# Top-k attention and SwiGLU block on one Trainium2 core: a parametric ReLU on ScalarE as the mask, normalization on GpSimd

## The chip, the cores and the metric

The kernel runs on one core of a Trainium2 chip. The metric is the device time of one execution in microseconds (us); lower is better. The engines are called by their short names: PE (TensorE, matrix products), ACT (ScalarE), DVE (VectorE), POOL (GpSimd) and SP (which issues most transfers).

## What is computed

Attention over 8 batches and 8 heads, 576 queries and keys of 64 numbers, in which each query keeps only its 32 highest scores, and then a SwiGLU feed-forward block (FFN) over the 4608 tokens. All in float32.

```python
# attention, q, k, v: (8, 8, 576, 64)
scores = scale * np.matmul(q, k.transpose(0, 1, 3, 2))      # scale = 1/8
kth = np.partition(scores, -32, axis=-1)[..., -32:-31]
scores = np.where(scores >= kth, scores, -1e9)
attn = np.exp(scores - scores.max(-1, keepdims=True))
attn = attn / (attn.sum(-1, keepdims=True) + 1e-9)
x = np.matmul(attn, v)                                      # to (4608, 512)
# FFN, w_gate and w_val (512, 1536), w_out (1536, 512)
g = x @ w_gate
out = (g * (1 / (1 + np.exp(-g))) * (x @ w_val)) @ w_out
```

## The kernel before

The attention is cut into 160 units: one unit is a batch, a tile of 128 queries and a pair of heads. 128 units have two heads of 128 queries each; in the last query tile of a batch (64 queries) both heads share the 128 partitions, so those 32 units count as one head. The order is by batch, then query tile, then pair of heads.

Each unit passes through these steps, all of them functions of the kernel:

- `scores` (L278): PE multiplies queries and keys into four PSUM banks (tile `s`, L308; L294 for the short units); ACT copies them to SBUF (tile `sc`, L313, L299).
- `select` (L316): for each head DVE takes the eight highest values four times (MAX8, L328) and between these rounds overwrites the ones found (MATCH_REPLACE8, L332). The 32 values stand in tile `m`, the 32nd in its last column. Then one instruction for each head compares the scores with that 32nd value and writes a penalty of -3e38 or 0 into tile `e` (L338).
- `penalize` (L342): POOL makes the bias of exp from the highest score (L348) and adds scores and penalty (L350).
- `weigh` (L353): ACT takes exp with the sum as a second output (L359) and adds a small constant to the sum, tile `tot` (L364).
- `normalize` (L367): DVE takes the reciprocal of the sum (L371), and ACT multiplies by it (L374).
- `turn` (L376): PE transposes the weights (tile `etps`, L386) and ACT copies them to `et` (L387).
- `values` (L397): PE multiplies with `v` for two units at once (tile `av`, L420); ACT copies the result into the FFN's input `xT` (L436).

The FFN is `feed` (L462), a generator that yields after each small piece of PE's work. It goes through 18 blocks of 256 tokens. Gate and value products (tile `f`, L476) go to PSUM; ACT evaluates them (L501 to L503, L508); POOL multiplies (L504, L509). The output product has two forms: a plain one for the first block (L522) and one of seven quarter products for the others (L562), with sums and differences on POOL (L548, L569, L577, L582, L610). A block can begin only when the attention of all its 256 tokens is done. The FFN's weights come in 36 pieces that are rounded on the way: a transfer that SP issues (L106), ACT (L114 to L117), DVE (L121), POOL (L122, L123).

The order on every engine is fixed by hand: at its end the kernel ties each instruction to the one before it on the same engine, so an engine never overtakes. That order is written by the main loop (L747), whose step n belongs to unit n. On DVE it runs `select(n)`. Around it stand `penalize(n - 1)` and `weigh(n - 1)`, `turn(n - 2)`, and in even steps the scores of units n + 1 and n + 2 and the values of units n - 4 and n - 3. The reciprocal of unit n - 1 comes at the end of step n, and the multiplication by it at the front of step n + 1, ahead of the copies of scores. Between these, `pieces` takes pieces of the FFN against a credit that `share` gives each step, and `dve` runs selection instructions and, with them, steps of the weights' rounding. All PSUM tiles of the attention (`s`, `av`, `etps`, `kqps`) share five banks in rotation; the FFN has three. `sc` and `e` have three buffers each, `m` two.

Of the kernel before, what the change touches and what calls it, by code (L numbers as in the profile page):

```python
# [8 lines left out]
AF = mybir.ActivationFunctionType  # L9
ALU = mybir.AluOpType  # L10
FP32 = mybir.dt.float32
# [4 lines left out]
P = 128  # L16
TOP_K = 32
LOWEST = -3.4028234663852886e38
FAR = -3.0e38
EPS = 1.0e-9  # L20
BLK = 256
WP = 256
# [3 lines left out]
def kernel(  # L26
# [66 lines left out]
    for i in range(NV):  # L93
        vt = consts.tile([P, P], FP32, name=f"vlast{i}")
        nc.vector.memset(vt[:], 0.0)
        vlast.append(vt)
    eps = consts.tile([P, 1], FP32, name="eps")
    nc.vector.memset(eps[:], EPS)
    wg = consts.tile([P, KC, DFF], FP32, name="wg")
    wv = consts.tile([P, KC, DFF], FP32, name="wv")  # L100
    wo = consts.tile([P, MC, DM], FP32, name="wo")
# [176 lines left out]
    def scores(n):  # L278
        b, qt, hp = units[n]
        slab = preps[b * NHP + hp]  # L280
        sc = work.tile([P, 2 * S], FP32, tag="sc", name="sc", bufs=3)
        halves = [slice(0, D), slice(D, P)]
        half = S // 2

        def bank():
            return ps_t.tile([P, 512], FP32, tag="t", name="s")


        if qt == J:
            banks = [bank() for _ in range(2)]  # L290
            for i, ps in enumerate(banks):
                for d in halves:
                    k0 = R + i * half
                    nc.tensor.matmul(  # L294
                        ps[d, 0:half], slab[d, S + R : S + 2 * R], slab[d, k0 : k0 + half]
                    )
            yield
            for i, ps in enumerate(banks):
                nc.scalar.copy(sc[:, i * half : (i + 1) * half], ps[:, 0:half])  # L299
        else:  # L300
            q0 = S + 2 * R + qt * P
            banks = []
            for i in range(2):
                for hh, d in enumerate(halves):
                    ps = bank()
                    banks.append((i + 2 * hh, ps))
                    k0 = (1 - hh) * R + i * half
                    nc.tensor.matmul(  # L308
                        ps[:, 0:half], slab[d, q0 : q0 + P], slab[d, k0 : k0 + half]
                    )  # L310
            yield
            for i, ps in banks:
                nc.scalar.copy(sc[:, i * half : (i + 1) * half], ps[:, 0:half])  # L313
        state[n] = dict(sc=sc)

    def select(n):  # L316

        nh = n_heads(units[n][1])
        sc = state[n]["sc"]
        m = small.tile([P, 2, TOP_K], FP32, tag="m", name="m", bufs=2)  # L320
        heads = [slice(t * S, (t + 1) * S) for t in range(nh)]
        e = work.tile([P, 2 * S], FP32, tag="e", name="e", bufs=3)
        state[n] |= dict(m=m, e=e, heads=heads)
# [2 lines left out]
        for r in range(rounds):  # L326
# [3 lines left out]
            if r < rounds - 1:  # L330
# [3 lines left out]
                    )  # L334
                    yield
                cur = e
        for t, hs in enumerate(heads):
            nc.vector.tensor_scalar(  # L338
                e[:, hs], sc[:, hs], m[:, t, TOP_K - 1 : TOP_K], FAR, ALU.is_lt, ALU.mult
            )  # L340

    def penalize(n):  # L342

        st = state[n]
        sc, m, e, heads = st.pop("sc"), st.pop("m"), st["e"], st["heads"]
        nh = len(heads)
        bias = small.tile([P, 2], FP32, tag="bias", name="bias")
        nc.gpsimd.tensor_scalar_mul(bias[:, 0:nh], m[:, 0:nh, 0], -scale)  # L348
        for hs in heads:
            nc.gpsimd.tensor_tensor(e[:, hs], e[:, hs], sc[:, hs], ALU.add)  # L350
        st["bias"] = bias

    def weigh(n):  # L353

        st = state[n]
        e, heads, bias = st["e"], st["heads"], st.pop("bias")
        tot = small.tile([P, 2], FP32, tag="tot", name="tot")
        for t, hs in enumerate(heads):
            nc.scalar.activation(  # L359
                e[:, hs], e[:, hs], AF.Exp, bias=bias[:, t : t + 1], scale=scale,  # L360
                accum_out=tot[:, t : t + 1],
            )
        nh = len(heads)
        nc.scalar.activation(tot[:, 0:nh], tot[:, 0:nh], AF.Identity, bias=eps[:])  # L364
        st["tot"] = tot

    def normalize(n):  # L367
        st = state[n]
        tot, e, heads = st.pop("tot"), st["e"], st.pop("heads")
        nh = len(heads)  # L370
        nc.vector.reciprocal(tot[:, 0:nh], tot[:, 0:nh])  # L371
        yield
        for t, hs in enumerate(heads):
            nc.scalar.mul(e[:, hs], e[:, hs], tot[:, t : t + 1])  # L374

    def turn(n):  # L376

# [340 lines left out]
    def pieces(n):  # L718
        for _ in range(n):
            if credit[0] >= 1:  # L720
                credit[0] -= piece()

    def run(steps):
        for _ in steps:
            pass
# [15 lines left out]
    load(2)  # L741
    credit = [0.0]
    no = iter(())
    scaled = no
    TURN = 2
    due = [2.0]
    for n in range(NU + 3):  # L747
# [6 lines left out]
        def dve(k, beside=True):  # L754

            for _ in range(k * nh):
                next(topk, None)
                due[0] += 5 / 6 if beside else 0
                if due[0] >= 1:
                    due[0] -= 1  # L760
                    rounding(1)
# [4 lines left out]
            credit[0] = min(credit[0] + share(n), share(n) + 1)  # L766
        flush(on_act)
        if 0 <= n - 1 < NU:
            penalize(n - 1)
        flush(on_pool)  # L770
        run(scaled)
        if nxt:
            run(nxt.pop(0))
        if valued(n):
# [27 lines left out]
        next(ahead, None)  # L802
        dve(1)
        pieces(1)
        dve(2, beside=False)
        run(topk)
        next(norm, None)
        scaled = norm
        pieces(6)
    while piece():  # L810
        pass
# [48 lines left out]
```

## Time and profile before

| | us |
|---|---|
| median of three runs (1789.26 to 1791.48) | 1791.11 |
| the profiled execution | 1790.76 |
| its span, first to last instruction | 1788.7 |
| PE busy | 1686.3 (94%) |
| DVE busy | 1619.7 (91%) |
| ACT busy | 1209.5 (68%) |
| POOL busy | 1068.0 (60%) |
| mean granted PE clock | 0.966 |

Busy time is the time in which an engine has an instruction in work, over the whole span. PE's granted clock is between 0.64 and 0.74 in the first 150 us, 0.93 from 300 to 400 us, and 0.98 or more in nearly all the rest. In the chain of work that ended last, 81% of the span are PE's, 9% DVE's and 4% POOL's. The transfers take little: 59.67 MB in all, 33 GB/s in the mean.

A row of the profile names the line of the kernel, the engine, the operation, and its tiles as output<-input, with shapes in partitions x elements. In a table of groups there follow busy time, mean ns of one instruction, and how long the engine was idle just before these, with what ended most of that idle time. In a timeline a row begins with its start and its length in us, and the number in brackets is the idle time before it.

### The profile page before, as it was taken

Reading aid. Unit: us, or ns where it says so; the run is one execution under the profiler, and the core shown is the slowest. Engines: PE = TensorE matmul, PEld = TensorE weight load, DVE = VectorE, ACT = ScalarE, POOL = GpSimd, SP = SyncE. Lnnn points to the kernel's source line nnn. Section 1 sums busy time; section 2 is a strip of 40 time slices with the busy share of each in tenths; the row PEclk is TensorE's granted clock in tenths of the full one; section 3 lists DMA queues with packets and bytes.
Section 4 is the critical chain, followed back from the end, with each engine's and each line's share of the span. In section 5 each row is a group of like instructions: output and inputs, shape, how many; then the busy total and the mean of one; then the engine's idle time right before and its main releaser. Section 6 shows DMA issues by size and latency. Waiting matters only on the chain.

```text
span 1788.7 us, 30860 instructions
## 1 busy us (share of the span) xinstructions
PE 1686.3 (94%) x11012; PEld 1396.2 (78%) x11012; DVE 1619.7 (91%) x3372; ACT 1209.5 (68%) x2881; POOL 1068.0 (60%) x1058
## 2 busy tenths in 40 slices
PE   4458999799999999999999999999999999999999
PEld 3337678588888888888888878888888878888877
DVE  7999999999999999999999989999999999999400
ACT  6788776667667677667666776767676776676431
POOL 4878856455565646564656646566556555756434
PEclk7669999899999999999999999999999999999989
DMA  7433030001200030001200030000300020000000
GB/s 193 126 96 95 32 75 14 13 1 36 60 1 13 3 80 15 12 1 35 62 13 1 13 71 26 1 13 6 90 1 13 1 55 15 13 1 13 1 12 12
DMA packets 109306, 59.67 MB, mean 33 GB/s; under 512 B 88544, under 2 KB 96992, under 8 KB 109152
## 3 DMA queue, kind: packets, MB, share of 16 engines
q1 hardware_dynamic: 108016, 57.37, 12.3%
q8 instruction: 87, 1.43, 0.3%
q14 instruction: 67, 0.55, 0.1%
q10 hardware_dynamic: 1136, 0.33, 0.1%
HBM read 48.23 MB, written 9.44 MB: 32 GB/s over the span
## 4 chain that ended last, share of the span: by engine, by line
PE 81%; DVE 9%; POOL 4%; ACT 3%; issue 2%; DMA 0%; SPq 0%; POOLq 0%; ACTq 0%; DVEq 0%
PE f L476 39%; PE x_ps L562 9%; PE av L420 8%; PE s L308 7%; PE etps L386 6%; PE y_ps L562 6%; DVE m L328 4%; DVE e L332 4%; PE s L294 2%; POOL e L350 1%; PE kqps L263 1%; PE o_ps L522 1%; DVE e L338 1%; DVE size L121 1%; ACT e L359 1%
## 5 line engine op out<-in xcount | busy, mean ns | idle before, releaser
L328 DVE MAX8 m<-e 128x8 f32<-128x576 f32 x864 | 614.5, 746 | 3.3
L350 POOL TENSOR_TENSOR e<-e,sc 128x576 f32<-128x576 f32 x288 | 408.7, 1437 | 111.8 <-DVE e L338 53.8
L332 DVE MATCH_REPLACE8 e<-m,e 128x576 f32<-128x576 f32 x576 | 423.3, 741 | 0.0
L476 PE MATMUL f<-xT,wg 128*128 128x256 f32 x1728 | 405.6, 384 | 0.0
L476 PE MATMUL f<-xT,wv 128*128 128x256 f32 x1728 | 399.6, 380 | 0.0
L476 PEld LDWEIGHTS f<-xT,wg 128*128 128x128 f32 x1728 | 326.4, 192 | 52.2 <-issue 8.9
L476 PEld LDWEIGHTS f<-xT,wv 128*128 128x128 f32 x1728 | 323.0, 190 | 49.1 <-issue 7.9
L504 POOL TENSOR_TENSOR h<-h,half_g 128x512 f32<-128x512 f32 x108 | 139.0, 1287 | 284.1 <-ACT h L503 274.5
L359 ACT ACTIVATE e<-e,bias 128x576 f32<-128x576 f32 x288 | 222.8, 778 | 79.0 <-POOL e L350 79.0
L509 POOL TENSOR_TENSOR h<-h,val 128x512 f32<-128x512 f32 x108 | 139.4, 1291 | 148.7 <-ACT val L508 147.9
L386 PE MATMUL etps<-ident,e 128*128 128x128 f32 (+1 forms) x1312 | 184.0, 284 | 45.7 <-ACT e L374 37.5
L374 ACT ACTIVATE e<-e,tot 128x576 f32<-128x576 f32 x288 | 210.9, 781 | 20.9 <-DVE tot L371 20.8
L308 PE MATMUL s<-kqT 64*128 64x288 f32 x1024 | 181.4, 461 | 41.9 <-ACT sc L313 27.6
L386 PEld LDWEIGHTS etps<-ident,e 128*128 128x128 f32 (+1 forms) x1312 | 157.5, 145 | 76.6 <-ACT e L374 41.4
L387 ACT COPY et<-etps 128x512 f32<-128x512 f32 (+1 forms) x448 | 182.5, 483 | 44.1 <-PE etps L386 44.0
L332 DVE MATCH_REPLACE8 e<-m,sc 128x576 f32<-128x576 f32 x288 | 211.5, 740 | 0.0
L328 DVE MAX8 m<-sc 128x8 f32<-128x576 f32 x288 | 202.5, 739 | 9.1 <-ACT sc L313 9.1
L338 DVE TENSOR_SCALAR e<-sc,m 128x576 f32<-128x576 f32 x288 | 185.4, 680 | 1.1
L313 ACT COPY sc<-s 128x288 f32<-128x288 f32 x512 | 164.9, 407 | 17.0 <-PE s L308 16.8
L308 PEld LDWEIGHTS s<-kqT 64*128 64x128 f32 x1024 | 102.6, 198 | 89.6 <-ACT sc L313 33.0
L420 PE MATMUL av<-et,v 128*64 128x128 f32 (+1 forms) x2560 | 158.6, 267 | 0.0
L501 ACT ACTIVATE h<-f 128x512 f32<-128x512 f32 x108 | 64.3, 595 | 116.8 <-PE f L476 116.6
(73 smaller groups left out, 2045.9 us busy)
## 6 DMA issues: line engine op xcount, KB each, us to landing
v<-in_v_dram SPq DMA_DIRECT2D x32, 256.0 KB, 3.2
kq_in<-in_k_dram SPq DMA_DIRECT2D x63, 128.0 KB, 2.9
kq_in<-in_q_dram SPq DMA_DIRECT2D x63, 128.0 KB, 3.1
w<-in_moe_w_gate_dram SPq DMA_DIRECT2D x12, 512.0 KB, 3.9
w<-in_moe_w_val_dram SPq DMA_DIRECT2D x12, 512.0 KB, 3.7
w<-in_moe_w_out_dram SPq DMA_DIRECT2D x12, 512.0 KB, 3.6
out_dram<-o SPq DMA_DIRECT2D x38, 128.0 KB, 2.4
out_dram<-o SPq DMA_DIRECT2D x16, 256.0 KB, 2.4
```

The source lines that it names most:

```text
L308: nc.tensor.matmul(ps[:, 0:half], slab[d, q0 : q0 + P], slab[d, k0 : k0 + half])
L328: nc.vector.max(m[:, t, 8 * r : 8 * r + 8], cur[:, hs])
L332: nc.vector.match_replace(e[:, hs], m[:, t, 8 * r : 8 * r + 8], cur[:, hs], LOWEST)
L338: nc.vector.tensor_scalar(e[:, hs], sc[:, hs], m[:, t, TOP_K - 1 : TOP_K], FAR, ALU.is_lt, ALU.mult)
L350: nc.gpsimd.tensor_tensor(e[:, hs], e[:, hs], sc[:, hs], ALU.add)
L359: nc.scalar.activation(e[:, hs], e[:, hs], AF.Exp, bias=bias[:, t : t + 1], scale=scale, accum_out=tot[:, t : t + 1],)
L374: nc.scalar.mul(e[:, hs], e[:, hs], tot[:, t : t + 1])
L386: nc.tensor.transpose(ps[0:kl, c * P : (c + 1) * P], e[:, k0 : k0 + kl], ident[:])
L387: nc.scalar.copy(et[0:kl, c0 : c0 + cn, :], ps[0:kl, 0 : cn * P].rearrange("p (c j) -> p c j", c=cn),)
L420: nc.tensor.matmul(av[d, i, 0:ql], weights_, moving, start=c == (0 if last else J), stop=c == (J if last else J - 1),)
L476: nc.tensor.matmul(ps[:, i, :], w[:, kc, m * P : (m + 1) * P], x[:, kc, :], start=(kc == 0), stop=(kc == KC - 1),)
L562: nc.tensor.matmul(ps, lhsT, T[i][m], start=m == 0, stop=m == MQ - 1)
```

## The change

A score x with the 32nd highest score t of its row is turned into t - x by ACT's input scaling, which is zero or negative where x is kept and positive where it is not. The parametric ReLU leaves positive values as they are and multiplies negative ones by 2^-90. exp then takes -2^90 times the result with a bias of t minus the highest score: kept scores come out as x minus the highest, and the others so far down that exp gives zero. The scale of 1/8 moves into the copies of scores.

With that, the comparison on DVE (L338), the addition on POOL (L350) and the constant's addition on ACT (L364) go. Two Prelu per unit come in on ACT ahead of exp; an addition of the constant for each head comes in on DVE ahead of the reciprocal; the multiplication by the reciprocal moves from ACT to POOL, with the reciprocal as a broadcast operand. In the main loop, the whole of `normalize(n - 1)` now runs within step n, ahead of the last two replacements and maxima of `select(n)`; before, its DVE part came at the end of step n and its multiplication at the front of step n + 1. POOL's bias instruction subtracts instead of multiplying. `m` gets three buffers. PE's instructions and their order stay as they are.

```diff
-FAR = -3.0e38
+SMALL = 2.0**-90
...
-    eps = consts.tile([P, 1], FP32, name="eps")
-    nc.vector.memset(eps[:], EPS)
...
# scores(n), in both branches
-                nc.scalar.copy(sc[:, i * half : (i + 1) * half], ps[:, 0:half])
+                nc.scalar.mul(sc[:, i * half : (i + 1) * half], ps[:, 0:half], scale)
...
# select(n)
-        m = small.tile([P, 2, TOP_K], FP32, tag="m", name="m", bufs=2)
+        m = small.tile([P, 2, TOP_K], FP32, tag="m", name="m")
...
-        for t, hs in enumerate(heads):
-            nc.vector.tensor_scalar(
-                e[:, hs], sc[:, hs], m[:, t, TOP_K - 1 : TOP_K], FAR, ALU.is_lt, ALU.mult
-            )
...
-    def penalize(n):
+    def shift(n):
...
-        nc.gpsimd.tensor_scalar_mul(bias[:, 0:nh], m[:, 0:nh, 0], -scale)
-        for hs in heads:
-            nc.gpsimd.tensor_tensor(e[:, hs], e[:, hs], sc[:, hs], ALU.add)
+        nc.gpsimd.tensor_tensor(
+            bias[:, 0:nh], m[:, 0:nh, TOP_K - 1], m[:, 0:nh, 0], ALU.subtract
+        )
...
# weigh(n)
         for t, hs in enumerate(heads):
             nc.scalar.activation(
-                e[:, hs], e[:, hs], AF.Exp, bias=bias[:, t : t + 1], scale=scale,
+                e[:, hs], sc[:, hs], AF.Prelu, bias=m[:, t, TOP_K - 1 : TOP_K], scale=-1.0,
+                alpha=SMALL,
+            )
+        for t, hs in enumerate(heads):
+            nc.scalar.activation(
+                e[:, hs], e[:, hs], AF.Exp, bias=bias[:, t : t + 1], scale=-1.0 / SMALL,
                 accum_out=tot[:, t : t + 1],
             )
-        nh = len(heads)
-        nc.scalar.activation(tot[:, 0:nh], tot[:, 0:nh], AF.Identity, bias=eps[:])
...
# normalize(n)
+        for t in range(nh):
+            nc.vector.tensor_scalar_add(tot[:, t : t + 1], tot[:, t : t + 1], EPS)
         nc.vector.reciprocal(tot[:, 0:nh], tot[:, 0:nh])
         yield
         for t, hs in enumerate(heads):
-            nc.scalar.mul(e[:, hs], e[:, hs], tot[:, t : t + 1])
+            nc.gpsimd.tensor_tensor(
+                e[:, hs], e[:, hs], tot[:, t : t + 1].to_broadcast([P, S]), ALU.mult
+            )
...
# the main loop
         if 0 <= n - 1 < NU:
-            penalize(n - 1)
+            shift(n - 1)
         flush(on_pool)
-        run(scaled)
         if nxt:
             run(nxt.pop(0))
...
         next(ahead, None)
         dve(1)
         pieces(1)
+        run(norm)
         dve(2, beside=False)
         run(topk)
-        next(norm, None)
-        scaled = norm
         pieces(6)
```

## The prediction

> **What bounds the kernel now.** I read the page's busy table first, then the table by stretches of time, then the timeline where that table shows TensorE idle. The busy table leaves two candidates:
>
> ```profile
> PE 1686.3 (94%) x11012; PEld 1396.2 (78%) x11012; DVE 1619.7 (91%) x3372; ACT 1209.5 (68%) x2881; POOL 1068.0 (60%) x1058
> ```
>
> The stretches separate them (columns: stretch, its length, busy us of PE, PEld, DVE, ACT, POOL, clock, DMA share, GB/s). I chose the cuts where PE fills up (137), runs dry (328) and fills up again (356).
>
> ```profile
> 0.00:137.00 137.00, 67.46 (x364) 46.90 (x364) 125.06 (x260) 102.23 (x227) 96.40 (x85) 0.68 0.51 139
> 137.00:328.00 191.00, 185.21 (x1158) 145.93 (x1158) 186.18 (x376) 141.60 (x331) 138.14 (x125) 0.98 0.17 48
> 328.00:356.00 28.00, 16.44 (x129) 11.95 (x128) 28.00 (x62) 17.42 (x48) 10.52 (x11) 0.81 0.05 20
> 356.00:1650.00 1294.00, 1285.96 (x8632) 1078.84 (x8633) 1257.08 (x2634) 901.88 (x2181) 760.48 (x773) 1.00 0.09 23
> ```
>
> Read it so: until 137 us, PE is half idle and DVE is never idle once it has data. There is no finished attention block, so PE has no FFN product to run, and DVE's selection sets the pace. From 356 to 1650 us, PE idles 8.0 of 1294 us while DVE idles 37. After DVE has ended, PE works alone for some 90 us. So PE sets the end, and time is to be won only where PE starves: 69.5 us idle in the first stretch, 5.8 in the second, 11.6 in the third.
>
> Next, what ends the starving in the first and the third stretch (the number in brackets is the engine's idle time before the row):
>
> ```profile
> 135.20 1.80 DVE L338 TENSOR_SCALAR e<-sc,m 128x576 f32<-128x576 f32 x2
> 136.92 0.15 DVE L371 RECIPROCAL tot<-tot 128x2 f32<-128x2 f32 x1
> 137.11 1.44 ACT L374 ACTIVATE e<-e,tot 128x576 f32<-128x576 f32 x2 [0.63 <-DVE tot L371]
> 138.46 1.28 ACT L313 COPY sc<-s 128x288 f32<-128x288 f32 x4
> 138.89 2.59 PE L308 MATMUL s<-kqT 64*128 64x288 f32 x8 [4.46 <-ACT sc L313]
> 141.40 4.94 PE L476 MATMUL f<-xT,wg 128*128 128x256 f32 x16
> ...
> 352.30 1.44 ACT L374 ACTIVATE e<-e,tot 128x576 f32<-128x576 f32 x2 [5.67 <-DVE tot L371]
> 354.07 1.71 PE L308 MATMUL s<-kqT 64*128 64x288 f32 x8 [3.63 <-ACT sc L313]
> ```
>
> One chain, twice: mask (L338), reciprocal at the loop's end (L371), ACT's multiplication (L374), the copies of scores behind it in ACT's queue (L313) that free PSUM banks, PE's next scores, and only then the first FFN product. The change removes the first link and moves the second and third.
>
> **What the Trainium skill says.** "ScalarE: Activation LUTs", What ACT_TABLE_LOAD costs: an ACTIVATE with a pointer bias takes about 280 + 0.833 N ns whatever the function, 760 ns at N = 576. The trace agrees: L359 (exp) 778 ns, L374 781 ns. "SBUF — State Buffer", Who interferes with whom: tensor_scalar can take the port pair that DVE shares with GpSimd, and the second comer blocks. The trace agrees: L338 takes 490 to 1611 ns, median 512, mean 680. "GPSIMD Engine Reference", 3.1: two-input elementwise work costs about 2.6 cycles per element, by my estimate 576 x 2.6 / 1.2 GHz = 1250 ns and a dispatch; L350 shows 1437 ns. "Perfetto Trace Analysis", Identifying the Most-Contended Engine, warns that matmul busy time is a poor measure of headroom. So I checked starts: the 16 products from 923.65 us give way to the next group at 927.21, 0.22 us each, and long runs of L476 elsewhere keep 0.216. PE really is full there.
>
> **The change, part by part.** The rows used:
>
> ```profile
> L350 POOL TENSOR_TENSOR e<-e,sc 128x576 f32<-128x576 f32 x288 | 408.7, 1437 | 111.8 <-DVE e L338 53.8
> L359 ACT ACTIVATE e<-e,bias 128x576 f32<-128x576 f32 x288 | 222.8, 778 | 79.0 <-POOL e L350 79.0
> L374 ACT ACTIVATE e<-e,tot 128x576 f32<-128x576 f32 x288 | 210.9, 781 | 20.9 <-DVE tot L371 20.8
> L338 DVE TENSOR_SCALAR e<-sc,m 128x576 f32<-128x576 f32 x288 | 185.4, 680 | 1.1
> ```
>
> *DVE.* Gone are 288 masks, 185.4 us. Added are 288 additions on 128x1. No such row exists; the nearest is the reciprocal on 128x1, 156 ns, behind which the next instruction starts after 0.08 us (136.92 to 137.00). A loop of two heads then pays 0.08 + 0.16 + 0.08 = 0.3 us for two additions and a reciprocal that waits for them; bounds 0.2 and 0.6. Before, mask to next loop took 1.80 us in even and about 1.15 in odd loops (135.20 to 137.00; 122.38 to 123.54), mean 1.47. Net: 1.17 us per loop, and ten loops (units 0 to 9) lie before the first FFN product. **Gain in stretch one: 11.7 us.** DVE's total should fall to about 1460 us; from 356 us on that buys nothing, since PE is the cover that hides it.
>
> *ACT.* Gone: 288 multiplications (210.9) and 160 Identity additions of eps (47.3). Added: 288 Prelu, taken as 778 ns (bounds 700 and 900), 224 us. Copies that become multiplications cost 8 ns more each (L502 594 against L508 586 ns), under 5 us, spread out. Sum: about 1180 us. The place matters more: the multiplication stood at the loop's front and waited for DVE's reciprocal, with the copies of scores queued behind. That wait goes. The copies can then run about 1.9 us earlier relative to DVE (138.89 against the loop's start at 137.00), though a weight piece's DMA may hold ACT there; I take 1.5 us, bounds 0 and 4. **Gain: 1.5 us.**
>
> *Third stretch.* PE runs dry for 2.5 loops; DVE's loops shrink by 1.1 us each, 2.7 us, and the chain at 352.30 loses its wait, of which I take 1.3. **Gain: 4 us,** bounds 0 and 9 (11.6 us are idle).
>
> *GpSimd.* 288 additions leave, 288 multiplications with a broadcast operand come; I take the same 1437 ns (bounds 1300 and 1600; L548's 512-wide broadcast addition takes 1377 ns against 1288 without). The bias instruction stays at about 260 ns. The work moves from the loop's front to its middle, so weight rounding (L122, L123, and SP's weight loads that wait for its buffers) starts earlier in a loop, and multiplications come after it. Nothing that PE needs soon stands behind them: the transposes of a unit come a loop later.
>
> *New waits.* DVE's addition waits mid-loop for ACT's exp; behind it are the last two replacements and last two maxima of the next unit. GpSimd's multiplication waits for DVE's reciprocal, with FFN products (L504, L509) and the next bias behind it. Either can cost PE only if it lasts about half a loop, 5 us. Closer is ACT's own queue in even loops:
>
> ```profile
> 922.77 0.42 ACT L436 COPY xT<-av 128x256 f32<-128x256 f32 x1
> 923.04 0.83 ACT L359 ACTIVATE e<-e,bias 128x576 f32<-128x576 f32 x1
> 924.75 0.30 ACT L364 ACTIVATE tot<-tot,eps 128x2 f32<-128x2 f32 x1
> 924.95 1.28 ACT L313 COPY sc<-s 128x288 f32<-128x288 f32 x4
> 927.21 1.15 PE L386 MATMUL etps<-ident,e 128*128 128x128 f32 x9
> ```
>
> Two Prelu (1.45 us) come between L436 and exp, L364 (0.2) goes: the copies end 1.25 us later where ACT was not waiting. PE's transposes need the first two of those banks; here they have 0.98 us to the last copy and some 1.2 more, since only the later transposes need them. In 10 of 63 such loops that distance is under 0.1 us; 10 x 0.2 = **2 us lost**, bounds 0 and 8. In the rest of stretches two and four PE idles 13.8 us, part of it behind waits that go: **2 us won**, bounds 0 and 4.
>
> The m buffers (2 to 3) and the missing memset move nothing: no wait on them shows. No DMA is added, and PE's program is the same instructions in the same order.
>
> **Sum:** 11.7 + 1.5 + 4 + 2 - 2 = 17.2 us. The profiled execution took 1790.76 us, span 1788.7 and 2.1 around it; 1790.8 - 17.2 = 1773.6, and the median shown lies 0.35 above that execution. I say 1774.
>
> **Rivals.** *(A) ACT's longer middle stalls PE: slower.* Place: the transposes (L386) in the 80 even loops, behind copies that come 1.25 us later. For it: some loops have no distance. Against: the median distance is near 1 us, and the multiplication's 1.4 us leaves ACT's queue ahead. It decides from 17 / 80 = 0.21 us lost per even loop; at 0.6 us it costs 48 - 2, so 1774 + 46 = 1820. A Prelu outside the loaded table is the same kind: two loads a loop at 1.28 us (the one ACT_TABLE_LOAD here), 320 x 1.28 = 410 us on ACT. But the changed program holds one load, as before.
> *(B) One wait replaces another: no change.* DVE reaches the new additions about 7.5 us after a loop's start (six maxima at 0.70, four replacements at 0.75, a weight step of 0.4); in the first stretch ACT has ahead of them copies (1.3 + 0.3), a weight piece (1.7), two Prelu (1.45) and two exps (1.9), 6.7 us and its start. If weight loads delay ACT by a microsecond, each loop gives its gain back: 1791 - 4 = 1787.
> *(C) More decoupling.* With ACT free of the reciprocal, PE runs ahead of DVE: 4 us instead of 1.5, 9 instead of 4, nothing lost: 1774 - 9.5 = 1764.
>
> **How the numbers follow.** A measurement of this kernel tells about 0.2%, 3.6 us, from no change. Forecast (1767 to 1783) 0.68; C (1757 to 1767) 0.10; B (1783 to 1794) 0.10; A (1795 to 1860) 0.12. Of B, about a fifth still counts as faster: faster 0.80, same 0.09, slower 0.11. The range 1763 to 1790 leaves out A, half of C and a little of B.
>
> **What would show it.** Right: the first FFN product at about 128 us, the second dry spell shorter by a third, DVE near 82% with its waits mid-loop on ACT, PE over 99% from 350 us on. Wrong: idle time of L386 behind ACT's copies in many loops (A), DVE's additions waiting over 1 us in loops 2 to 9 (B), Prelu far from 778 ns, or the broadcast multiplication over 1600.

## The result, and the profile after

Between repeated runs the changed kernel takes **1779.61 us** (median; 1776.86 to 1781.56), the kernel before 1791.3 us on the same chip: ratio 0.9935, interval 0.9918 to 0.9953, so 11.7 us or 0.65% less (the interval holds the true ratio with 95% confidence). The forecast was 1774 us, in a range of 1763 to 1790. The profiled execution took 1778.34 us with a span of 1776.6; against the profiled execution before (1790.76 and 1788.7) the span is 12.1 us shorter, and this is the difference that I take apart below.

The busy table of the changed kernel, the line that answers to the first one shown of before:

```profile
PE 1679.1 (95%) x11012; PEld 1386.4 (78%) x11012; DVE 1483.2 (83%) x3371; ACT 1163.2 (65%) x2721; POOL 959.5 (54%) x1058
```

DVE lost 136.5 us of work, and the kernel became 12 us shorter: some nine tenths of what was removed had been hidden behind TensorE, or were given back elsewhere. The same stretches as before (stretch, its length, busy us of PE, PEld, DVE, ACT, POOL, clock, DMA share, GB/s) show where it counted and where not:

```profile
0.00:137.00 137.00, 74.04 (x398) 51.68 (x399) 121.95 (x279) 108.37 (x239) 90.09 (x86) 0.70 0.52 143
137.00:328.00 191.00, 183.48 (x1181) 142.25 (x1180) 166.59 (x367) 134.94 (x312) 124.21 (x124) 1.00 0.17 47
328.00:356.00 28.00, 23.30 (x136) 18.70 (x137) 27.90 (x66) 18.24 (x46) 9.85 (x11) 0.82 0.01 5
356.00:1650.00 1294.00, 1278.47 (x8647) 1069.98 (x8646) 1148.59 (x2622) 863.15 (x2050) 675.15 (x771) 1.00 0.09 23
```

PE idles less in the first and the third stretch (63.0 and 4.7 us, before 69.5 and 11.6), but in the long one it now idles 15.5 us where it idled 8.0. Something is given back there.

The chain that was shown of before, at the end of the first and of the second starving, in the timeline of the changed kernel (start, duration, then the row; in square brackets the idle time before it):

```profile
125.16 0.20 DVE L369 TENSOR_SCALAR tot<-tot 128x1 f32<-128x1 f32 x2
125.40 0.17 DVE L370 RECIPROCAL tot<-tot 128x2 f32<-128x2 f32 x1
...
128.98 2.24 POOL L373 TENSOR_TENSOR e<-e,tot 128x576 f32<-128x576 f32 x2
129.07 1.30 ACT L311 ACTIVATE sc<-s 128x288 f32<-128x288 f32 x4
130.65 1.24 PE L306 MATMUL s<-kqT 64*128 64x288 f32 x8
...
131.82 1.35 PE L477 MATMUL f<-xT,wg 128*128 128x256 f32 x5
...
333.00 2.43 PE L387 MATMUL etps<-ident,e 128*128 128x128 f32 x9 [3.27 <-POOL e L373]
...
343.66 3.72 PE L477 MATMUL f<-xT,wg 128*128 128x256 f32 x16
```

The mask is gone, the reciprocal lies in the loop's middle, and the copies of scores (L311) no longer stand behind a multiplication. The first FFN product starts at 131.82 instead of 141.40 us.

The costs of the new rows, in the table of groups (busy us, mean ns of one, idle before it):

```profile
L373 POOL TENSOR_TENSOR e<-e,tot 128x576 f32<-128x576 f32 x288 | 325.1, 1148 | 120.9 <-DVE tot L370 106.5 <-ACT et L388 4.5 <-PE etps L387 3.9
L358 ACT ACTIVATE e<-e,bias 128x576 f32<-128x576 f32 x288 | 220.3, 767 | 75.7 <-POOL bias L341 73.3 <-ACT e L353 0.4
L353 ACT ACTIVATE e<-sc,m 128x576 f32<-128x576 f32 x288 | 210.3, 778 | 7.4 <-DVE m L326 7.1
L369 DVE TENSOR_SCALAR tot<-tot 128x1 f32<-128x1 f32 x288 | 36.5, 146 | 198.7 <-ACT e L358 198.7
```

**The same instruction in both traces.** TensorE executes the same matmuls in the same order in both kernels. So the k-th matmul of one trace can be set against the k-th of the other, and the difference of their starts says how much has been won up to there. A change of that difference has a place (each column comes from one trace of its kernel):

| matmul | before, us | after, against before |
|---|---|---|
| first FFN product | 141.40 | -9.6 |
| just ahead of the second dry spell | 316.8 | -7.7 |
| after the dry spell | 375 | -13.6 |
| ahead of the loss shown below at 1540 | 1520 | -12.7 |
| near the end of the long stretch | 1668 | -8.7 |
| last matmul | 1784.6 | -12.2 |

Five steps: 9.6 won, 1.9 lost, 5.9 won, 4.9 lost, 3.4 won in the tail; together 12.2. The 4.9 are a net figure: around 1070 us 2.3 us are won, where the kernel before had a pause of 2.21 us. The experiments ask for the cause of each.

### The profile page after: what moved, and what is told of

It is laid out like the page before. It is cut to its first block, busy times and chain, and to the rows that moved or that the text cites. A ratio compares the mean times of both kernels' runs of the same rounds, so it can differ in the third digit from the quotient of the medians.

```text
span 1776.6 us, 31074 instructions
## 1 busy us (share of the span) xinstructions
PE 1679.1 (95%) x11012; PEld 1386.4 (78%) x11012; DVE 1483.2 (83%) x3371; ACT 1163.2 (65%) x2721; POOL 959.5 (54%) x1058
## 4 chain that ended last, share of the span: by engine, by line
PE 77%; POOL 7%; DVE 7%; ACT 5%; issue 3%; SPq 1%; DMA 1%; POOLq 0%; ACTq 0%; DVEq 0%
PE f L477 38%; PE av L421 9%; PE x_ps L563 8%; PE s L306 6%; PE etps L387 6%; PE y_ps L563 6%; DVE m L326 3%; DVE e L330 3%; POOL e L373 2%; ACT e L358 2%; PE s L292 2%; PE kqps L261 1%; PE o_ps L523 1%; ACT e L353 1%; POOL h L510 1%
## 5 line engine op out<-in xcount | busy, mean ns | idle before, releaser
L477 PE MATMUL f<-xT,wg 128*128 128x256 f32 x1728 | 401.2, 381 | 0.0
L373 POOL TENSOR_TENSOR e<-e,tot 128x576 f32<-128x576 f32 x288 | 325.1, 1148 | 120.9 <-DVE tot L370 106.5
L353 ACT ACTIVATE e<-sc,m 128x576 f32<-128x576 f32 x288 | 210.3, 778 | 7.4 <-DVE m L326 7.1
L311 ACT ACTIVATE sc<-s 128x288 f32<-128x288 f32 x512 | 167.4, 414 | 63.2 <-PE s L306 62.7
L306 PE MATMUL s<-kqT 64*128 64x288 f32 x1024 | 174.5, 453 | 30.5 <-ACT et L388 17.4
L369 DVE TENSOR_SCALAR tot<-tot 128x1 f32<-128x1 f32 x288 | 36.5, 146 | 198.7 <-ACT e L358 198.7
L388 ACT COPY et<-etps 128x512 f32<-128x512 f32 (+1 forms) x448 | 182.5, 485 | 26.1 <-PE etps L387 26.1
L306 PEld LDWEIGHTS s<-kqT 64*128 64x128 f32 x1024 | 95.9, 195 | 78.5 <-issue 26.3
L421 PEld LDWEIGHTS av<-et,v 128*64 128x64 f32 x2560 | 140.3, 142 | 7.0 <-issue 3.6
```

Of the source, the lines that this page charges most:

```text
L306: nc.tensor.matmul(ps[:, 0:half], slab[d, q0 : q0 + P], slab[d, k0 : k0 + half])
L311: nc.scalar.mul(sc[:, i * half : (i + 1) * half], ps[:, 0:half], scale)
L353: nc.scalar.activation(e[:, hs], sc[:, hs], AF.Prelu, bias=m[:, t, TOP_K - 1 : TOP_K], scale=-1.0, alpha=SMALL,)
L373: nc.gpsimd.tensor_tensor(e[:, hs], e[:, hs], tot[:, t : t + 1].to_broadcast([P, S]), ALU.mult)
L388: nc.scalar.copy(et[0:kl, c0 : c0 + cn, :], ps[0:kl, 0 : cn * P].rearrange("p (c j) -> p c j", c=cn),)
L421: nc.tensor.matmul(av[d, i, 0:ql], weights_, moving, start=c == (0 if last else J), stop=c == (J if last else J - 1),)
```

## The experiments

**Theory:** TensorE sets the end. What is won before the first FFN product stays to the end one for one; in the steady state DVE's shorter loop is worth nothing as long as it stays under TensorE's; and the multiplication, now in GpSimd's in-order queue, delays FFN sums and transposes there. **Rivals:** DVE's time counts everywhere; or ACT's longer middle is what gives time back.

The change and all twelve experiments, with the time before measured beside these at 1790.5 to 1791.1 us:

| kernel | median us | ratio to before, interval |
|---|---|---|
| the change | 1779.61 | 0.9935 (0.9918 to 0.9953) |
| mask_new_norm | 1874.88 | 1.0470 (1.0456 to 1.0484) |
| prelu_old_norm | 1786.67 | 0.9982 (0.9973 to 0.9992) |
| dead10 | 1795.52 | 1.0027 (1.0017 to 1.0037) |
| max_first10 | 1782.29 | 0.9954 (0.9940 to 0.9967) |
| late1 | 1776.06 | 0.9915 (0.9902 to 0.9929) |
| dead32 | 1852.48 | 1.0349 (1.0332 to 1.0366) |
| max_from32 | 1783.08 | 0.9953 (0.9941 to 0.9966) |
| mul_dve32 | 1787.78 | 0.9979 (0.9972 to 0.9986) |
| prelu_twice | 1816.40 | 1.0137 (1.0122 to 1.0153) |
| late1_bias | 1780.62 | 0.9948 (0.9935 to 0.9960) |
| late1_sums | 1772.95 | 0.9901 (0.9888 to 0.9915) |
| late_dry | 1778.10 | 0.9930 (0.9917 to 0.9944) |

An interval reaches 1 to 3 us to either side. Where two rows differ by no more than that, the totals don't settle it, and what is said below rests on the place where their matmuls part. Line numbers in the profile of an experiment are its own; an edit shifts them by up to six.

### One half of the change at a time

mask_new_norm: the kernel before, with the new normalization.

```diff
-        nc.scalar.activation(tot[:, 0:nh], tot[:, 0:nh], AF.Identity, bias=eps[:])
+        for t in range(nh):
+            nc.vector.tensor_scalar_add(tot[:, t : t + 1], tot[:, t : t + 1], EPS)
         nc.vector.reciprocal(tot[:, 0:nh], tot[:, 0:nh])
...
-            nc.scalar.mul(e[:, hs], e[:, hs], tot[:, t : t + 1])
+            nc.gpsimd.tensor_tensor(
+                e[:, hs], e[:, hs], tot[:, t : t + 1].to_broadcast([P, S]), ALU.mult)
...
+        run(norm)
         dve(2, beside=False)
         run(topk)
-        next(norm, None)
-        scaled = norm
```

> The other half: mask and penalty as before, the normalization as in the change (additions on VectorE, multiplication on GpSimd, in the middle of the loop). PE-theory: VectorE's loops are 0.2 us longer, GpSimd has additions and multiplications both (near 1400 us busy), so stalls behind it grow: 1791 to 1800 us, no gain. Rival (the moved normalization gains by freeing ScalarE from the wait for the reciprocal): 1778 to 1784 us.

prelu_old_norm: the changed kernel with the three edits above reversed.

> Half of the change: the mask by Prelu, but the normalization as before (constant added on ScalarE, reciprocal at the loop's end, multiplication on ScalarE at the front of the next loop). PE-theory: loops before the first product are 1.3 us shorter and the wait in loop 1 is gone, so the first product comes at 128 to 130 us; the dry spell keeps ScalarE's wait for the reciprocal and gains only 2 to 3 us; the small stalls behind GpSimd's multiplication are gone, 4 to 6 us. Sum 1774 to 1779 us, no slower than the whole change. Rival (the moved normalization is what gains): 1788 us or more.

Both expectations were missed. The halves alone are worth +84 and -4.3 us, together -11.7: they can't be costed apart. In mask_new_norm GpSimd has additions and multiplications (busy 1403 us), the mask takes longer beside them (882 ns in the mean, 680 before), and DVE's full loops last 11.73 us against 11.00 before. In prelu_old_norm ACT carries Prelu and the multiplication (busy 1387.8 us, 78%). Its first FFN product comes at 132.70, nearly as early as in the change, but at 236 us it is 3.9 us behind the change, and at the end 6.9. Of TensorE's waits after 356 us 15.6 of 18.1 us are then for ACT; in the change ACT has 5.6 of 15.0.

### Does what is won before the first FFN product stay?

dead10 and dead32: the changed kernel with masks into a scratch tile that nobody reads, at the place of the old ones, in units 0 to 9, and from unit 32 on.

```diff
...
                 cur = e
+        if n < 10:    # dead32: n >= 32
+            for hs in heads:
+                nc.vector.tensor_scalar(
+                    dead[:], sc[:, hs], m[:, 0, TOP_K - 1 : TOP_K], -3.0e38, ALU.is_lt, ALU.mult)
```

> The changed kernel with the two masks per unit put back as dead work on VectorE, into a scratch tile, for units 0 to 9 only. PE-theory (TensorE sets the end; VectorE's saving counts only before the first FFN product and in the dry spell): the first FFN product comes 10 us later than in the changed kernel and the whole gain but some 2 to 4 us is lost, 1786 to 1790 us. DVE-theory (VectorE sets the pace in every loop and the change loses elsewhere what it gains): ten of 144 full loops lose 1.2 us each less what is hidden, at most 12 us lost as well in the first stretch, but then the run of dead masks from unit 32 on must lose ten times that; taken alone this run does not tell the two apart.

> The changed kernel with the same dead masks for units 32 to 159 only (some 230 masks, about 150 us of VectorE work). PE-theory: 0 to 4 us lost, 1780 to 1784 us, and VectorE's idle time in the middle of the loops shrinks by about 150 us. DVE-theory: up to 1.2 us for each of about 115 full loops, 1850 to 1910 us.

dead10 came 16 us above the change: more than expected, in the theory's direction. dead32 broke the theory as I had it: 73 us slower where 0 to 4 were expected, and at 1852 us inside the range of the rival, by which DVE's time counts everywhere. The table of one tile shows the first reason (ns: least, median, most):

```profile
L338 DVE TENSOR_SCALAR dead<-sc,m x20: 499/1084/1284, 22.1 to 144.3; 128x576 f32<-128x576 f32 x20
```

```profile
L338 DVE TENSOR_SCALAR dead<-sc,m x228: 499/868/1601, 373.9 to 1767.7; 128x576 f32<-128x576 f32 x114
```

A mask costs 0.5 us where GpSimd is quiet. At the loop's end it now meets the new multiplication or FFN sums, so a pair adds about 2 us to a loop (1.7 to 2.3 in dead10). That is the rule of the Trainium skill ("SBUF — State Buffer", Who interferes with whom: a tensor_scalar may take the shared pair, the later comer blocks), and the trace agrees, 499 to 1601 ns. The second reason is TensorE's pace, which I had put too high. It is about 11.1 us a loop: the mean of full loops from unit 40 on is 11.00 before and 11.11 after, while an undisturbed loop of DVE takes 10.56 and 9.95. With two more microseconds, DVE's loop (11.9) passed TensorE's. A dose without collisions was needed to tell the two apart.

max_first10 and max_from32: one dead MAX8 a unit instead, which reads one operand; late1: the one loop ahead of the first FFN product in which DVE had waited for more than 0.3 us gets its normalization at the end.

```diff
...
+        if n < 10:    # max_from32: n >= 32
+            nc.vector.max(dead[:], sc[:, heads[0]])
         rounds = TOP_K // 8
```

```diff
-        run(norm)
+        if n != 1:
+            run(norm)
         dve(2, beside=False)
         run(topk)
+        run(norm)
```

> The changed kernel with one further MAX8 of 128x576 (into a scratch tile, read by nobody) in each of units 0 to 9: about 0.73 us of DVE a loop before the first FFN product, without the collision on the port shared with GpSimd that the dead masks had. Theory (the gain is made of DVE's time before the first product, one for one to the end): first product 7.3 us later, 139.1; time 1786 to 1788. Rival (the weights' DMAs or ACT set the pace of the first stretch by now and cover it): 1780 to 1783.

> The changed kernel with one further MAX8 of 128x576 (scratch, read by nobody) in each unit from 32 on: 0.73 us of DVE a loop, 128 times, in all 93 us, with no collision on the shared port. Theory (a loop of TensorE takes about 11.3 us, DVE's 9.95 + 0.73 = 10.7 stays under it): 1779 to 1784. Rival (DVE's saved time counts in the steady state too; the dead masks from unit 32 on cost 73 us for that reason, not because they took DVE over TensorE's pace): 1830 to 1873.

> The changed kernel, but with the additions, the reciprocal and the multiplication of step 1 put at the loop's end instead of its middle (in all other steps unchanged). In the changed kernel DVE's two additions waited 1.95 + 0.60 us for exp there, and it is the only loop of the first ten in which they waited. Theory (what is lost before the first FFN product stays to the end, one for one): the wait goes, the first product comes 2.5 us earlier than 131.8, the time falls by 2 to 3 us to about 1777. Rival (the wait only took the place of another one later in the loop, for example the weights' DMA): the first product and the time stay, 1779 to 1780.

The wait that late1 removes, in the changed kernel's timeline:

```profile
31.51 1.46 ACT L353 ACTIVATE e<-sc,m 128x576 f32<-128x576 f32 x2
32.85 0.79 ACT L358 ACTIVATE e<-e,bias 128x576 f32<-128x576 f32 x1
33.51 0.21 ACT L358 ACTIVATION_READ_ACCUMULATOR e<-e,bias 128x1 f32 x1
33.60 0.79 ACT L358 ACTIVATE e<-e,bias 128x576 f32<-128x576 f32 x1
...
33.76 0.15 DVE L369 TENSOR_SCALAR tot<-tot 128x1 f32<-128x1 f32 x1 [1.95 <-ACT e L358]
34.52 0.15 DVE L369 TENSOR_SCALAR tot<-tot 128x1 f32<-128x1 f32 x1 [0.60 <-ACT e L358]
```

The additions wait for the accumulators of two exps, and exp is late because ACT had two weight pieces ahead of it. In late1 the first product comes at 128.96 us, 2.86 earlier; at the last matmul the distance is 2.64, and the time 3.5 us less. Of the 2.86, 2.2 lie in the loop that was edited and 0.7 in the one ahead of it, which holds the same instructions. Loops 0 and 1 together take 23.7 to 24.4 us in the four traces with this edit and 26.6 to 27.1 in five without: the edit is worth 2.7 us there. In max_first10 it comes 3.97 us later and the last matmul 3.94; the time rises by 2.7. In dead10 it is 14.1 us at the first product, 14.3 to 14.9 from 160 to 1640 us and 17.4 at the end, after the tail. So what is won or lost ahead of the first product stays to the end, as the theory says. Only the size in max_first10 was off, 4 instead of 7.3: a MAX8 adds 0.66 us to a loop, not 0.73, and in loops 0 and 1 it mostly filled DVE's wait for exp.

max_from32 gave DVE 83 us more to do and cost 3.5 us: DVE's time in the steady state is hidden, and the rival (1830 to 1873) is out.

### What is the steady state's cover worth?

mul_dve32: from unit 32 on, DVE multiplies.

```diff
         for t, hs in enumerate(heads):
+            if n >= 32:
+                nc.vector.tensor_scalar_mul(e[:, hs], e[:, hs], tot[:, t : t + 1])
+                continue
             nc.gpsimd.tensor_tensor(
```

> The changed kernel, but from unit 32 on the multiplication by the reciprocal is done by DVE (two tensor_scalar of about 0.5 us a unit) instead of GpSimd. Theory (TensorE sets the end, a full loop of it is about 11.3 us, and the 6 to 7 us lost after 356 us come from multiplications that stand behind FFN sums in GpSimd's queue): DVE's loop grows from 9.95 to about 11.0 us, still under 11.3, the stalls of the transposes behind GpSimd's multiplication go, 1773 to 1777. Rival 1 (those losses have another cause, ACT's copies or the PSUM banks): 1779 to 1782. Rival 2 (DVE's time from 356 us on sets the end, or the multiplication collides with GpSimd's work on the shared port as the dead mask did, so that the pair takes over 1.4 us): 1790 to 1860.

Missed: 1787.78. The multiplication takes 659 ns on DVE in the mean, not 500, though 520 in the median: some of them last up to 1592 ns, as the masks did beside GpSimd. TensorE's waits for GpSimd's multiplication after 356 us vanish, but those for its subtractions (L611 of the change) rise from 1.4 to 6.8 us and for ACT's copies of the transposes (L388) from 2.3 to 8.0. Four kernels can be set side by side. DVE's loop is the mean of those full loops, from unit 40 on, in which DVE waits for nothing; the delay of TensorE is that between matmul 1500 and matmul 10500, against the change:

| kernel | DVE busy, us | DVE's loop, us | loops without a wait, of 96 | TensorE's delay, us |
|---|---|---|---|---|
| the change | 1483.2 | 9.95 | 52 | 0 |
| max_from32 | 1566.3 | 10.61 | 64 | 4.8 |
| mul_dve32 | 1617.8 | 11.23 | 93 | 10.0 |
| dead32 | 1682.4 | 11.85 | 92 | 72.3 |

Up to 10.6 us the cover holds. In mul_dve32 and dead32 DVE hardly waits any more, its loop is over TensorE's 11.1, and by these figures it is DVE that sets the pace. This is no clean curve: the four edits differ in more than DVE's time, for mul_dve32 takes work off GpSimd, and collisions lengthen its loop and that of dead32.

Nor are max_from32's 4.8 us a price by the loop: all of them arise in one place. Around 1063 us in its timeline (the edit shifts the lines by three: L376, L581 and L586 are L373, L578 and L583 of the change):

```profile
1058.59 2.09 POOL L581 TENSOR_TENSOR h<-h 128x256 f32<-128x256 f32 x3
1062.98 2.25 POOL L376 TENSOR_TENSOR e<-e,tot 128x576 f32<-128x576 f32 x2 [2.30 <-DVE tot L373]
1065.18 1.41 POOL L586 TENSOR_TENSOR xT<-h 128x256 f32<-128x256 f32 x2
...
1065.97 4.51 PE L566 MATMUL y_ps<-t,xT 128*128 128x256 f32 x12 [3.22 <-POOL xT L586]
```

GpSimd stands idle for 2.30 us because its next instruction, the multiplication (L376), waits for DVE's reciprocal; the FFN subtraction behind it (L586) was ready, and TensorE waits 3.22 us for that. In the change this wait lasts 1.2 us at the same place. The twelve products behind it then take 4.51 us, where 2.75 is usual, for TensorE's clock falls to half after the pause (more of that below, in the second dry spell).

### Is it GpSimd's queue that gives time back?

After 356 us TensorE's waits in the kernel before, and in the changed kernel (us, times, longest):

```profile
PE x_ps L562 <- POOL xT L569: 2.7, 2, 2.2
...
PE x_ps L562 <- POOL h L577: 1.2, 2, 0.6
PE etps L386 <- ACT sc L313: 1.1, 3, 0.8
...
PE etps L386 <- ACT e L374: 0.4, 1, 0.4
```

```profile
PE etps L387 <- POOL e L373: 4.7, 10, 0.9
PE etps L387 <- ACT sc L311: 3.3, 5, 0.7
PE y_ps L563 <- POOL xT L583: 2.1, 2, 1.2
...
PE x_ps L563 <- POOL h L611: 1.4, 2, 0.9
```

GpSimd's queue already held TensorE before, by 3.9 us, with the subtractions and sums of the FFN; with the multiplication in it the waits for GpSimd are 8.8 us. Those for ACT rise from 3.7 to 5.6 us.

Where TensorE lost most, at 1540 us, the timeline of the changed kernel reads:

```profile
1533.71 0.61 ACT L597 COPY p<-y_ps 128x512 f32<-128x512 f32 x1
...
1534.39 0.73 POOL L549 TENSOR_TENSOR p<-p 128x256 f32<-128x256 f32 x1 [7.99 <-ACT p L597]
...
1537.12 2.10 POOL L611 TENSOR_TENSOR h<-h,xT 128x256 f32<-128x256 f32 x3
1539.19 2.25 POOL L373 TENSOR_TENSOR e<-e,tot 128x576 f32<-128x576 f32 x2
...
1540.39 0.66 PE L387 MATMUL etps<-ident,e 128*128 128x128 f32 x4 [0.92 <-POOL e L373]
```

A sum (L549) waits 8 us for ACT's copy of y_ps. Behind it stand two more sums, three subtractions (L611), and the multiplication, whose reciprocal had been ready at 1533.0. late1_sums has late1's edit and changes that order, nothing else: the three sums that depend on L597 go behind L611 and L373.

```diff
-            on_pool.append(sum_up)
+            later.append(sum_up)
...
         def rest_y():
             nc.scalar.copy(o[:, 0, left], y_ps2[:])
+            flush(later)
...
             shift(n - 1)
         flush(on_pool)
+        flush(later)
```

> The changed kernel with the normalization of step 1 at the loop's end (as in late1), and with the three sums of an FFN block that wait for ACT's copy of y_ps put behind the subtractions of the next quarter and the attention's multiplication in GpSimd's queue (same instructions, other order). Theory (the 5 to 7 us that the changed kernel loses again after 356 us come from GpSimd's in-order queue: multiplications and subtractions stand behind sums that wait for ACT): the waits of TensorE for the multiplication fall from 4.7 us to under 1.5, and for the subtractions from 1.4 to under 0.5; time 1771 to 1774. Rival (the queue is only where the wait shows; TensorE would stop a little later for ACT's copies anyway): 1775 to 1777, as late1.

1772.95 us, as the theory expected, 3.1 below late1. The intervals of the two overlap (0.9888 to 0.9915 and 0.9902 to 0.9929), so the totals alone would not prove it; the waits and the place of the gain do. The waits after 356 us:

```profile
PE etps L387 <- ACT sc L311: 3.3, 5, 0.7
PE etps L387 <- POOL e L373: 2.8, 7, 0.5
PE y_ps L563 <- POOL xT L583: 2.1, 2, 1.2
```

The wait for L611 is gone; that for the multiplication fell to 2.8 us, not under 1.5. Between 1065 and 1672 us this kernel wins 4.4 us on late1. It would have shown more, had its first product not come 1.9 us later (130.91) with the same instructions in the first ten loops. The traces place that in the weights' transfers: ACT waited 2.33 us for one of them (until 48.74 us; in late1 1.09), exp came later, and in loops 3 and 4, together 1.6 us longer, DVE's additions waited for exp as they had in loop 1 of the change. In the tail it lost 1.5 us to a longer spell of the low clock. This kernel has the lowest time of all, 0.9901 of before.

late1_bias, also with late1's edit, tries the other suspect in that queue, the bias, behind which exp waits 73 us.

```diff
-        nc.gpsimd.tensor_tensor(
+        (nc.vector if n >= 12 else nc.gpsimd).tensor_tensor(
             bias[:, 0:nh], m[:, 0:nh, TOP_K - 1], m[:, 0:nh, 0], ALU.subtract
```

> The changed kernel with the normalization of step 1 at the loop's end, and with the bias of exp (a subtraction on 128x2) on DVE instead of GpSimd from step 12 on. Theory (GpSimd's queue holds exp back through the bias, 73 us of ACT's waiting, but mostly where TensorE doesn't need exp soon): ACT's wait for the bias goes, TensorE's idle time after 356 us falls by 0 to 2 us; time 1774 to 1777. Rival (exp held back by the bias is the cause of the loss after 356 us): 1769 to 1772. DVE's loop grows by about 0.2 us and stays under TensorE's 11.3.

Both expectations missed: 1780.62, slower than late1 by 4.6. ACT's wait for the bias goes (1.2 us are left of 73), and TensorE's waits for the multiplication stay (4.8 us), so exp held back by the bias is not what loses time. But the edit is no clean test of the total: the subtraction takes 0.6 us on DVE (159 to 1206 ns) instead of 0.2, which adds 81 us to DVE and lengthens its loop by 0.7 us to 10.6, as in max_from32. The same wait as there grew, that for L583, from 2.1 to 3.6 us. Of the rest, 1.3 us arose in the tail.

### ACT's longer middle

prelu_twice: a second, dead Prelu behind each from unit 32 on.

```diff
...
                 alpha=SMALL,
             )
+            if n >= 32:
+                nc.scalar.activation(dead[:], sc[:, hs], AF.Prelu,
+                    bias=m[:, t, TOP_K - 1 : TOP_K], scale=-1.0, alpha=SMALL)
```

> The changed kernel with each Prelu from unit 32 on followed by a second one into a scratch tile that nobody reads: 1.45 us more of ACT between the copies of attention sums and exp in each full unit, about 180 us in all. Theory of the forecast (two more Prelu in ACT's middle lie within the distance that the transposes leave, a second pair of them doesn't): copies of scores reach the transposes too late in many even loops, 0.2 to 0.6 us each in some 50 of them, 1790 to 1810. Rival (ACT's place in the loop has more room than that, and costs nothing until ACT as a whole is full, which at 65% + 10% it isn't): 1779 to 1784.

1816.4 us, 37 above the change and beyond the expectation, although ACT is far from full. TensorE's longest waits after 356 us:

```profile
PE etps L393 <- ACT sc L312: 13.9, 19, 1.2
PE etps L393 <- POOL e L379: 9.2, 16, 1.2
PE kqps L262 <- ACT et L394: 5.5, 3, 2.0
```

So the distance between ACT's copies and the transposes is real, and the change has used most of it: 1.45 us more, and the copies are late in 19 loops instead of 5. The multiplication, which waits for exp through the reciprocal, slips with them. Rival A of the forecast is right as a mechanism; the first pair of Prelu stays nearly inside. TensorE's idle time explains some 22 of the 37 us; spells of the low clock, of which three lie in the middle of this trace and none in that of the change, have a part in the rest, which I have not taken apart.

### The second dry spell

late_dry: late1, with the normalization at the loop's end also in steps 27 to 30.

```diff
-        run(norm)
+        if n != 1 and not 27 <= n <= 30:
+            run(norm)
...
+        run(norm)
```

> The changed kernel with the normalization at the loop's end in step 1 (as in late1) and in steps 27 to 30, the loops around the second dry spell of TensorE; DVE's loops keep their length. Theory (the gain in the dry spell is more than forecast because the multiplication now starts in the loop's middle, some 2.6 us earlier, while the transposes of a unit wait for it there: 3.3 us behind the multiplication in the changed kernel, 5.3 before): of the 5.9 us gained there 2 to 3 go, 1778 to 1779.5. Rival (the gain there comes from DVE's shorter loops alone, as forecast): 1775.5 to 1776.5, as late1.

1778.10, within the theory's numbers, but only half for its reason: through the dry spell TensorE loses 1.1 us against late1 (its wait for the multiplication is 4.92 us instead of 3.27), and 1.6 more come in the tail. And prelu_old_norm, which has the old place, wins 5.9 us there, as much as the change. So the place of the multiplication is worth 1 us, and DVE's shorter loops are most of the gain, as forecast. Where the forecast's size was short is seen at the end of the spell. Before, behind the pause of 3.63 us at 354.07:

```profile
355.72 5.29 PE L476 MATMUL f<-xT,wg 128*128 128x256 f32 x16
...
1718.43 1.33 PE L386 MATMUL etps<-ident,e 128*128 128x128 f32 x5 [3.70 <-ACT e L374]
...
1722.61 6.21 PE L476 MATMUL f<-xT,wg 128*128 128x256 f32 x16
```

After a pause of 3.6 to 3.7 us, sixteen products take 5.29 and 6.21 us. Without one just before they take 3.72 (at 343.66 in the changed kernel, shown above). The granted clock shows why. Three stretches of the kernel before and one of the changed kernel:

```profile
1068.92:1072.33 3.41, 1.20 (x8) 0.88 (x7) 3.41 (x9) 2.04 (x7) 3.41 (x5) 1.00 0.46 104
1072.33:1075.74 3.41, 3.41 (x9) 2.70 (x9) 3.41 (x8) 0.00 (x0) 3.41 (x6) 0.50 0.00 0
1717.45:1727.69 10.24, 9.26 (x57) 7.42 (x58) 0.00 (x0) 1.93 (x6) 0.00 (x0) 0.50 0.06 13
```

```profile
1710.48:1713.89 3.41, 3.41 (x29) 2.75 (x26) 0.00 (x0) 0.27 (x1) 0.00 (x0) 0.50 0.00 0
```

In the traces of all fourteen kernels the clock is either full or half, and after 137 us every spell at half lasts 3.41, 6.83, 10.24 or 13.65 us, one to four steps of 3.41. A spell begins at the end of such a step, often when TensorE is at work again: ahead of each one TensorE had been busy for at most 2.05 of the last 3.41 us, and wherever it had been busy for less than 1.48 us, a spell followed. So a pause of 2.21 us brought one (ahead of 1071.61 in the kernel before), and one of 2.41 us (ahead of 182.51) did not. The Trainium skill describes it ("TensorE: Matmul & The Clock Gate", Part 1): an idle window of about 3.4 us halves the clock, and a busy one of that length restores it. The traces agree on the half and on 3.4 us as the step, but a window needn't be wholly idle, and at 1717.45 three of them passed before the clock came back, though TensorE worked without a pause from 1718.43 on. A removed pause is thus worth its length and more: between 354.7 and 361 us of the kernel before, where it has a spell of 3.41 us and the change has none, TensorE's lead in the change grows by 2.0 us with no wait at all. In the tail, too, the last unit's wait shrank in the change, and the spell was shorter, 3.41 instead of 10.24 us:

```profile
1708.97 0.77 PE L387 MATMUL etps<-ident,e 128*128 128x128 f32 x5 [2.97 <-POOL e L373]
...
1712.01 4.64 PE L477 MATMUL f<-xT,wg 128*128 128x256 f32 x16
```

How long it lasts is in part chance. late_dry has the same pause there, 2.98 us, but a spell of 6.83 us and 5.98 us for the sixteen products; late1_sums and late1_bias have 6.83 us too, late1 3.41. This one step is the 1.3 to 1.6 us by which these three fall behind late1 in the tail.

## Why the prediction was nearly right

The time was 5.6 us above the forecast and inside the range; direction and place held. The span fell by 12.1 where the sum had 17.2. That it came so near is in part luck: 5.4 us of the gain, the clock in the third stretch and the tail, were not in the sum, and without them 6.7 would be left. Of the signs named in advance, DVE's share (83%), its waits mid-loop on ACT (198.7 us at L369) and the dry spell shorter by a third (11.6 to 7.2 us idle) came; the first FFN product at 128 us and TensorE over 99% (98.8 from 356 us on) did not. Step by step:

- **DVE, 11.7 us before the first product, "ten loops".** The price was right, one loop count wrong. Loops 2 to 9 shrank by 1.13 us each, forecast 1.17. Loops 0 and 1 together grew by 0.4 instead of shrinking by 2.3, because DVE's additions waited 1.95 + 0.60 us for exp. That is rival B, in one loop of ten; late1's edit gives 2.7 us of it back.
- **ACT released, 1.5 us.** From DVE's start of unit 10 to the first product 3.6 us instead of 4.4: 0.8. Together with the step above 9.6 of 13.2; in late1 12.4.
- **Third stretch, 4 us.** 5.9, inside the bounds. Its mechanism was right; the clock after the pause, some 2 us, was not in the sum.
- **ACT's longer middle, 2 us lost.** The waits behind ACT's copies after 356 us rose from 1.1 to 3.3 us. Right, and prelu_twice shows how near the edge was.
- **Other idle time, 2 us won; "Nothing that PE needs soon stands behind them"; a wait of GpSimd "can cost PE only if it lasts about half a loop".** This step failed. 1.9 us were lost ahead of the dry spell and 4.9 after it. Ahead of it 3.9 of TensorE's 4.9 us of waits were for GpSimd (before, 3.7 us, all for ACT). After 356 us the waits for GpSimd's queue (L373, L583, L611, L570) rose from 3.9 to 8.8 us, those for ACT from 3.7 to 5.6. A multiplication that waits 2.3 us for its reciprocal is enough, when an FFN subtraction stands behind it; and the multiplication itself can stand behind an FFN sum. I had followed DVE's and ACT's queue through a loop, but not GpSimd's through an FFN block. late1_sums gives 4.4 us of it back by order alone.
- **The tail, not in the sum.** 3.4 us won: a pause shortened from 3.70 to 2.97 us, and a shorter spell of the low clock after it, of which one step is chance.
- **"From 356 us on that buys nothing".** Right, but the cover was thinner than the text let one think: 11.1 us against DVE's 9.95 (before, 10.56 in the median and, with the collisions, 10.85 in the mean).
- **Prices.** Prelu 778 ns, as taken. Two additions and a reciprocal delay DVE's next instruction by 0.32 us (125.16 to 125.48), 0.3 taken. GpSimd's multiplication took 1148 ns, under the lower bound of 1300.

Left open: which transfers of the weights come late in a run, and with it the scatter of the first product (128.96 to 130.91 us in four kernels with late1's edit, 130.68 to 132.10 in five with the change's own first stretch); and the part of prelu_twice's loss that idle time doesn't explain.

## What to carry to other kernels

To cost an instruction that moves to an in-order queue, walk that queue over the longest period of its work (here an FFN block, not a loop): what stands before it and waits, and what stands behind it while it waits. Set an engine's loop, its collisions included, against the loop of the engine that hides it; the difference, not the busy share, says how much may be moved there, and two edits that share a port or an engine have no separate prices. Comparing the k-th matmul of two traces gives every gain and loss its place, which a total can't.

## What the runs showed of the hardware

- GpSimd's multiplication of 128x576 by a broadcast column takes 1148 ns, an addition of two full 128x576 operands 1437 (L350 before). In mask_new_norm, which has both, the medians are 1147 and 1409 ns. A broadcast over the middle axis isn't cheaper: 1273 ns at 128x512, 1274 without (L549 of the change).
- The same mask on DVE takes 499 to 1601 ns, by what GpSimd does meanwhile; a MAX8 of the same size 735 to 764 (changed kernel).
- A subtraction of operands of 128x2 or 128x1 takes 159 to 1206 ns on DVE beside GpSimd's work (late1_bias), 183 to 387 ns on GpSimd (the change).
- Pauses of TensorE of 1.9 us (prelu_old_norm, up to 174.43 us) and more were followed by half the clock, for 3.41 us or two to four times that, where they fell so that TensorE was busy for at most 2.05 of 3.41 us; sixteen 128x256 products took 4.64 to 6.21 us instead of 3.6 to 3.7. Of two traces with the same pause of 2.98 us one had 3.41 us of it (late1), the other 6.83 (late_dry).
